# A decode step of attention and MLP on one core: the query weights loaded ahead of the MLP weights, and the queries made ahead of the MLP

## The chip, the cores and the metric

The kernel runs on one core of a Trainium2 chip. A core has five engines with their own instruction streams: TensorE (PE in the profile, its weight loads PEld), VectorE (DVE), ScalarE (ACT), GpSimd (POOL) and SyncE (SP), and 16 DMA engines that serve the queues of all of them. An engine takes its instructions in order; semaphores tie the engines together. The metric is the device time in microseconds.

## What is computed

One token x of 512 values is normalised, and two branches read the result xn. Branch A is attention over a cache: 32 heads of 128 values, each with its own keys and values, of which the last 4096 positions count. Branch B is a small MLP. The output is x plus the product of both.

```python
W = min(4096, max(256, Sk // 4))                 # 4096 of 32768 positions
q = (xn @ wq) per head                           # wq: 512 x 4096
p = softmax(q . k[:, Sk - W:, :] * 128 ** -0.5)
A = concat(p @ v[:, Sk - W:, :]) @ wo            # wo: 4096 x 512
h  = gelu(layernorm(xn) @ w1)
hs = concat(shifted quarters of h) @ w2          # one position only: every shift leaves zeros
x1 = xn + hs
B  = x1 + gelu(layernorm(x1) @ w3) @ w4          # w3: 512 x 1376, w4: 1376 x 512
out = x + A * silu(B)
```

With one position, the four shifts move h out of the sequence, so hs is a product of zeros with w2; the kernel carries it out with a zero vector. All tensors are bfloat16. Keys and values in the window are 32 MB each, wq and wo 4 MB each, the MLP weights 3.3 MB.

## The kernel before

**Loads.** All large loads are issued by SP through `load` (L77), which keeps them in program order. x comes twice through the ACT queue: `x_bf` (L81), spread over 128 partitions, and `x_row` (L84), four rows. SP issues w2, w3, w4 in three pieces, then wq (L85 to L94), each row of a partition contiguous: 4 KB for w2, 11 KB for w3, 32 KB for wq. Then follow, in a loop over pairs of heads s = 0 to 18, K of pair s (2 MB, a tile of 64 x 128 values in each partition) and V of pair s - 3. K has six buffers, V three. The V buffers lie where the weights were: the pool `wts` (w2, w3, w4, wq, and small tiles such as `sel`, `q_rows` and `hr`) is closed at s = 3 (L530), so the load of V0 waits until everything in `wts` has been read. As SP takes its instructions in order, K4 and all later loads stand behind V0.

**Ahead of the loop.** The statistics of x (`ln_stats`, L155: two products with a matrix of ones, short VectorE steps, a power on GpSimd) give `xn_f` and `xn_bf` (L179 to L185). The MLP follows: hs from w2 (L194), x1, the second statistics, `z3_bf` (L200), `a_ps` from w3 in 44 matmuls of one column (L212), Gelu on ScalarE, `hr_ps` in 15 matmuls of 512 columns with w2 and w4 (L220 and L223), a copy `hr`, the spreading over four rows `h2_ps` (L228 and L229), `bv`, and Silu into `g_row` (L233), which is used at the very end (L612). Then the queries: `qT_ps` in 128 matmuls of one column (L239), a transpose, `q_rows`, and `q_bc`, the queries of each pair spread over all partitions by four groups of four matmuls and four ScalarE copies (L248 to L253).

**In the loop.** Scores are made in two ways that share each K tile: of its 64 chunks of positions VectorE takes 32 or 40 in two halves (`k_vector`: the product with `q_bc`, L313, and a sum, L315), and TensorE the rest (`k_turn`: transposes, L328, which ScalarE copies, L329; `k_scores`, L334). The softmax works on two pairs at a time (`sm_*`), `v_pair` makes the weighted sums of the values (L431, L442), and the product with wo is gathered in `y_ps`. The loop is a region whose order on TensorE, VectorE and ScalarE is that of the program text. The instructions ahead of it are ordered by the scheduler, which may mix independent ones; the small masks and constants of L132 to L293 are put into gaps on VectorE in this way. All instructions ahead of the region come first on these three engines.

`ps_misc`, the PSUM pool of the MLP's and the queries' small results, has a single buffer, so each of them waits until the one before it has been read.

Of the kernel before, what the change touches and what calls it, by code (L numbers as in the profile page):

```python
# [8 lines left out]
P = 128  # L9
BF16 = mybir.dt.bfloat16  # L10
FP32 = mybir.dt.float32
# [18 lines left out]
def kernel(  # L30
# [14 lines left out]
    nc = tc.nc  # L45
# [3 lines left out]
    _, H, Sk, Dh = A_k_cache.shape  # L49
    HD = A_wq.shape[1]  # L50
# [5 lines left out]
    KC = D // P  # L56
# [9 lines left out]
    small = ctx.enter_context(tc.tile_pool(name="small", bufs=1))  # L66
    ps_misc = ctx.enter_context(tc.tile_pool(name="ps_misc", bufs=1, space=PSUM))
    ps_tr = ctx.enter_context(tc.tile_pool(name="ps_tr", bufs=3, space=PSUM))
# [6 lines left out]
    wts = wts_guard.__enter__()  # L75

    def load(dst, src):  # L77
        return tc.keep_in_program_order(nc.sync.dma_start(out=dst, in_=src))  # L78
# [3 lines left out]
    x_row = small.tile([P, P], BF16, name="x_row")  # L82
    nc.gpsimd.memset(x_row[:], 0.0)
    nc.scalar.dma_start(out=x_row[0:P:32, :], in_=A_x.rearrange("a b (j n) -> (a b j) n", j=KC))  # L84
    w2_sb = wts.tile([P, KC, D], BF16, name="w2_sb")  # L85
    load(w2_sb[:], B_w2.rearrange("(p c) n -> p c n", p=P))
    w3_sb = wts.tile([P, KC, F], BF16, name="w3_sb")
# [2 lines left out]
    load(w4_sb[:, 0:8, :], B_w4[0:8 * P, :].rearrange("(p c) n -> p c n", p=P))  # L90
    load(w4_sb[:, 8:10, :], B_w4[8 * P:10 * P, :].rearrange("(p c) n -> p c n", p=P))
    load(w4_sb[0:96, 10, :], B_w4[10 * P:F, :])
    wq_sb = wts.tile([P, KC, HD], BF16, name="wq_sb")
    load(wq_sb[:], A_wq.rearrange("(p c) n -> p c n", p=P))  # L94

    def load_kv(pool, cache, i, cuts=None):
        t = pool.tile([P, CP, Dh], BF16, tag="kv", name="kv")
# [9 lines left out]
    ident_bf = const.tile([P, P], BF16, name="ident_bf")  # L107
# [11 lines left out]
    sel = wts.tile([H, H // 2, P // 2, 2], BF16, name="sel")  # L119
# [9 lines left out]
    def make_masks(n):  # L129
        m = P // n  # L130
        blk = const.tile([P, m], BF16, name=f"blk{n}")
        nc.vector.tensor_reduce(out=blk[:], in_=ident_bf[:].rearrange("d (i t) -> d i t", t=n),  # L132
                                axis=AX.X, op=ALU.max)
        to = const.tile([P, n, m], BF16, name=f"to{n}")
        nc.vector.tensor_copy(out=to[:], in_=blk[:].unsqueeze(1).to_broadcast([P, n, m]))
        mt = const.tile([P, n], BF16, name=f"mt{n}")
        nc.vector.tensor_reduce(out=mt[:], in_=ident_bf[:].rearrange("d (i t) -> d t i", t=n),
                                axis=AX.X, op=ALU.max)
        mh = const.tile([P, n], FP32, name=f"mh{n}")
        nc.vector.tensor_reduce(out=mh[:], in_=ident_bf[:].rearrange("d (h i) -> d h i", h=n),  # L140
                                axis=AX.X, op=ALU.max)
        masks[n] = (to, mt, mh)
# [41 lines left out]
    xn_bf = small.tile([P, KC], BF16, name="xn_bf")  # L184
    nc.vector.tensor_copy(out=xn_bf[:], in_=xn_f[:])  # L185

    shifted_bf = small.tile([P, KC], BF16, name="shifted_bf")
    nc.vector.memset(shifted_bf[:], 0.0)  # L190
    hs_ps = ps_misc.tile([P, KC], FP32, tag="misc", name="hs_ps")
    for j in range(KC):
        for c in range(KC):
            nc.tensor.matmul(hs_ps[:, j:j + 1], lhsT=w2_sb[:, c, j::4],  # L194
                             rhs=shifted_bf[:, c:c + 1], start=(c == 0), stop=(c == KC - 1))
# [14 lines left out]
    for j, (m, cols) in enumerate(chunks):  # L210
        for c in range(KC):
            nc.tensor.matmul(a_ps[0:m, j:j + 1], lhsT=w3_sb[:, c, cols], rhs=z3_bf[:, c:c + 1],  # L212
                             start=(c == 0), stop=(c == KC - 1))
# [5 lines left out]
    for c in range(KC):  # L219
        nc.tensor.matmul(hr_ps[:], lhsT=shifted_bf[:, c:c + 1], rhs=w2_sb[:, c, :], start=(c == 0),  # L220
                         stop=False)
    for i, (m, _) in enumerate(chunks):
        nc.tensor.matmul(hr_ps[:], lhsT=a_bf[0:m, i:i + 1], rhs=w4_sb[0:m, i, :], start=False,  # L223
                         stop=(i == len(chunks) - 1))
# [7 lines left out]
    g_row = small.tile([P, P], FP32, name="g_row")  # L232
    nc.scalar.activation(out=g_row[:], in_=bv[:], func=ACT.Silu)  # L233


    qT_ps = ps_misc.tile([P, H], FP32, tag="misc", name="qT_ps")
    for h in range(H):
        for c in range(KC):
            nc.tensor.matmul(qT_ps[:, h:h + 1], lhsT=wq_sb[:, c, h * Dh:(h + 1) * Dh],  # L239
                             rhs=xn_bf[:, c:c + 1], start=(c == 0), stop=(c == KC - 1))  # L240
    qT_bf = small.tile([P, H], BF16, name="qT_bf")
    nc.vector.tensor_copy(out=qT_bf[:], in_=qT_ps[:])
    qr_ps = ps_misc.tile([H, Dh], BF16, tag="misc", name="qr_ps")
    nc.tensor.transpose(qr_ps[:], qT_bf[:], ident_bf[:])
    q_rows = wts.tile([H, Dh], BF16, name="q_rows")
    nc.vector.tensor_copy(out=q_rows[:], in_=qr_ps[:])
    q_bc = small.tile([P, H // 2, Dh], BF16, name="q_bc")
    for i in range(0, H // 2, 4):  # L248
        qb_ps = ps_tr.tile([P, 4, Dh], FP32, tag="pt", name="qb_ps")
        for k in range(4):  # L250
            nc.tensor.matmul(qb_ps[:, k, :], lhsT=sel[:, i + k, :, :].rearrange("k b a -> k (b a)"),
                             rhs=q_rows[:], start=True, stop=True)
        nc.scalar.copy(out=q_bc[:, i:i + 4, :], in_=qb_ps[:])  # L253
    make_masks(16)
    make_masks(8)

# [4 lines left out]
    for c in range(2):  # L261
        nc.vector.tensor_copy(
            out=few[:, c, 0:4 * NE].rearrange("p (a b) -> p a b", b=4),
            in_=ident_bf[:, 4 * NE * c:4 * NE * (c + 1)].rearrange("p (b a) -> p a b", b=4))
# [27 lines left out]
    for r in range(2):  # L292
        nc.vector.tensor_copy(out=pick_f[:, :, r, :],  # L293
                              in_=ident_bf[:, 32 * r:32 * r + 8].rearrange("p (i a) -> p i a", a=2))
# [230 lines left out]
    for s in range(NP + LAG):  # L525
        h = s - LAG
# [119 lines left out]
```

## Time and profile before

| | |
|---|---|
| median of 5 runs | 195.45 us (195.42 to 196.69) |
| profiled execution | 195.44 us, span of the core 193.6 us |
| busy share of the span: PE / DVE / ACT / POOL | 70% / 75% / 41% / 3% |
| DMA: bytes, queue of SP | 78.84 MB, 96.1% of 16 engines |
| chain that ended last | DMA 40%, DVE 37%, PE 11%, issue 3%, SP queue 3%, ACT 2% |

The span runs from the core's first instruction to its last; the rest of a run's time lies around it. In the profile's rows of slices each digit is the busy share of one fortieth of the span in tenths, and GB/s is what the DMA engines moved in it. A line of the timeline has start, duration, engine, line of the kernel, operation, output and inputs, and in brackets how long the engine stood idle before it and what ended that. A line of a DMA issue ends with the time from issue to landing. q1 is the queue of SP's loads, q10 that of ACT's.

### The profile page before, as it was taken

What the parts mean: (1) busy time and instruction counts of PE and PEld (TensorE: products, weight loads), DVE (VectorE), ACT (ScalarE), POOL (GpSimd) and SP (SyncE); (2) the same over time, 40 slices, a digit from 0 to 9 for tenths busy, and PEclk for the clock granted to TensorE, in tenths of its full rate; (3) what the DMA queues carried; (4) which work ended last, traced back from release to release, by engine and by line L of the source; (5) the groups of instructions that cost most, each with busy time, mean ns of one, the idle gap of its engine ahead of it and who ended that gap; (6) DMA issues with size and microseconds to landing.
All of it is one profiled execution on the core that took longest, in us unless ns stands there. A gap on an engine that the chain in (4) does not pass through costs nothing.

```text
span 193.6 us, 4727 instructions
## 1 busy us (share of the span) xinstructions
PE 136.4 (70%) x2108; PEld 105.4 (54%) x2108; DVE 145.3 (75%) x164; ACT 79.0 (41%) x173; POOL 6.2 (3%) x13
## 2 busy tenths in 40 slices
PE   0549779762687699497969944857757897958751
PEld 0444369652686663335959432247747546956640
DVE  1550108999999999999999999499999977792001
ACT  2003009882855460537359153161545028833000
POOL 2210006000000000000000000000000000000000
PEclk9999955975555556969555995795555579555555
DMA  6999899999999999999999999999999999999970
GB/s 211 407 507 433 372 427 433 430 422 427 433 427 427 427 418 430 427 433 433 427 430 423 430 430 430 430 433 423 427 433 427 433 428 432 416 437 416 411 309 3
DMA packets 7051, 79.13 MB, mean 409 GB/s; under 512 B 888, under 2 KB 1752, under 8 KB 2264
## 3 DMA queue, kind: packets, MB, share of 16 engines
q1 hardware_dynamic: 6880, 78.84, 96.1%
q8 instruction: 16, 0.26, 0.5%
q10 hardware_dynamic: 152, 0.00, 0.0%
q14 instruction: 3, 0.02, 0.0%
HBM read 78.84 MB, written 0.00 MB: 407 GB/s over the span
## 4 chain that ended last, share of the span: by engine, by line
DMA 40%; DVE 37%; PE 11%; issue 3%; SPq 3%; ACT 2%; POOL 1%; DVEq 0%; POOLq 0%
DMA kv<-in_A_k_cache_dram 31%; DVE S L315 22%; DVE prod L313 12%; DMA wo_rows<-in_A_wo_dram 7%; SPq L78 3%; PE hr_ps L223 2%; DMA x_bf<-in_A_x_dram 2%; ACT kt L329 2%; PE qT_ps L239 2%; PE oT L442 2%; PE a_ps L212 1%; PE oT L449 1%; PE hr_ps L220 1%; PE pt L328 1%; POOL ln_rstd_x L175 0%
## 5 line engine op out<-in xcount | busy, mean ns | idle before, releaser
L315 DVE TENSOR_REDUCE S<-prod 128x20 f32<-128x2560 bf16 (+1 forms) x32 | 83.8, 2620 | 1.1
L329 ACT COPY kt<-pt 128x1024 bf16<-128x1024 bf16 x54 | 51.0, 1021 | 22.8 <-PE pt L328 22.8
L313 DVE TENSOR_TENSOR prod<-kv,q_bc 128x2560 bf16<-128x2560 bf16 (+1 forms) x32 | 44.3, 1385 | 6.9 <-DMA kv<-in_A_k_cache_dram 4.6
L328 PE MATMUL pt<-ident_bf,kv 128*128 128x128 bf16 x432 | 40.2, 273 | 7.2 <-DMA kv<-in_A_k_cache_dram 5.3
L328 PEld LDWEIGHTS <-kv 128*128 128x128 bf16 x432 | 36.3, 127 | 10.7 <-DMA kv<-in_A_k_cache_dram 6.4
L442 PE MATMUL oT<-pT,kv 128*128 128x2 bf16 x768 | 22.5, 165 | 4.1 <-DMA kv<-in_A_v_cache_dram 4.1
L334 PE MATMUL sT<-qT_bf,kt 128*128 128x2 bf16 x432 | 17.5, 166 | 10.5 <-ACT kt L329 10.1
L442 PEld LDWEIGHTS <-kv 128*128 128x128 bf16 x768 | 21.6, 104 | 5.5 <-DMA kv<-in_A_v_cache_dram 5.4
L334 PEld LDWEIGHTS <-kt 128*128 128x128 bf16 x432 | 16.1, 104 | 13.1 <-ACT kt L329 12.3
L431 PE MATMUL ov<-kv,pT 128*8 128x512 bf16 x64 | 19.9, 481 | 0.0
L431 PEld LDWEIGHTS <-pT 128*8 128x8 bf16 x64 | 6.3, 103 | 12.3 <-issue 8.6
L371 PE MATMUL mb_ps<-md,par_t 4*128 4x4 f32 x16 | 4.3, 336 | 12.2 <-DVE md L363 12.2
L378 ACT ACTIVATE pT<-S,mb 128x64 bf16<-128x64 f32 x32 | 10.9, 357 | 0.2
L374 ACT COPY mb<-mb_ps 128x4 f32<-128x4 f32 x8 | 1.3, 162 | 23.2 <-PE mb_ps L371 23.2
L371 PEld LDWEIGHTS mb_ps<-md,par_t 4*128 4x128 f32 x16 | 3.8, 290 | 12.8 <-issue 12.2
L462 DVE TENSOR_TENSOR o<-oT,rden 128x2 bf16<-128x2 f32 x3 | 0.5, 160 | 10.7 <-PE oT L442 10.7
L466 ACT ACTIVATE o<-oT,rden 128x1 bf16<-128x1 f32 x26 | 4.7, 264 | 7.3 <-PE oT L449 5.3
L226 DVE COPY hr<-hr_ps 1x512 f32<-1x512 f32 x1 | 0.7, 679 | 8.8 <-PE hr_ps L223 8.8
L359 PE MATMUL mt_ps<-ident_f,m 128*2 128x128 f32 x8 | 2.8, 353 | 5.2 <-DVE m L353 5.2
L507 PE MATMUL yr_ps<-wo,ox 128*1 128x512 bf16 x16 | 6.1, 564 | 0.0
L378 ACT ACTIVATION_READ_ACCUMULATOR pT<-S,mb 128x1 f32 x32 | 6.0, 187 | 0.0
L157 PE MATMUL ln_ps<-x_f,ones_f 128*128 128x4 f32 x4 | 1.2, 365 | 5.9 <-DVE x_f L180 4.8
(116 smaller groups left out, 95.1 us busy)
## 6 DMA issues: line engine op xcount, KB each, us to landing
kv<-in_A_k_cache_dram SPq DMA_DIRECT2D x16, 2048.0 KB, 29.0
kv<-in_A_v_cache_dram SPq DMA_DIRECT2D x15, 2048.0 KB, 26.0
wq_sb<-in_A_wq_dram SPq DMA_DIRECT2D x1, 4096.0 KB, 17.7
wo<-in_A_wo_dram SPq DMA_DIRECT2D x1, 2048.0 KB, 27.1
w_sb<-in_B_w_dram SPq DMA_DIRECT2D x1, 1376.0 KB, 6.6
w_sb<-in_B_w_dram SPq DMA_DIRECT2D x1, 1024.0 KB
wo<-in_A_wo_dram SPq DMA_DIRECT2D x1, 1024.0 KB, 26.9
kv<-in_A_v_cache_dram SPq DMA_DIRECT2D x1, 1024.0 KB
```

Source lines behind the costliest of these rows:

```text
L78: return tc.keep_in_program_order(nc.sync.dma_start(out=dst, in_=src))
L313: nc.vector.tensor_tensor(out=prod[:, 0:m, :], in0=kn[:, rows, :], in1=q_bc[:, s:s + 1, :].to_broadcast([P, m, Dh]), op=ALU.mult)
L315: nc.vector.tensor_reduce(out=st[s // 2]["S"][:, s % 2, rows], in_=prod[:, 0:m, :], axis=AX.X, op=ALU.add)
L328: nc.tensor.transpose(pt[:, i, :], kn[:, n + b + i, :], ident_bf[:])
L329: nc.scalar.copy(out=kts[s][:, b:b + w, :], in_=pt[:, 0:w, :])
L334: nc.tensor.matmul(st[s // 2]["sT"][:, s % 2, c, :], lhsT=kt[:, c, :], rhs=qT_bf[:, 2 * s:2 * s + 2], start=True, stop=True)
L371: nc.tensor.matmul(mb_ps[:], lhsT=par_t[:].rearrange("k b a -> k (b a)"), rhs=md[:].rearrange("k r a -> k (r a)"), start=True, stop=True)
L378: nc.scalar.activation(out=s["pT"][:, i // 2, :, i % 2], in_=s["S"][:, i // 2, :], func=ACT.Exp, scale=scale, bias=mb[:, i:i + 1], accum_o ...
L431: nc.tensor.matmul(s["ov"][32 * r:32 * r + 8], lhsT=s["pT"][:, r, c:c + 4, :].rearrange("p i a -> p (i a)"), rhs=v[:, c:c + 4, :], start=F ...
L442: nc.tensor.matmul(s["oT"][:, 2 * r:2 * r + 2], lhsT=v[:, c, :], rhs=s["pT"][:, r, c, :], start=(c == 0), stop=(c == CP - 1))
L466: nc.scalar.mul(o_blk[b][:, c + k:c + k + 1], st[g]["oT"][:, hl + k:hl + k + 1], st[g]["rden"][:, hl + k:hl + k + 1])
L507: nc.tensor.matmul(yr_ps[:], lhsT=ox_blk[i][:, t:t + 1], rhs=wo_blk[i][:, t, :], start=(t == 0), stop=(t == n - 1))
```

## The change

Two blocks of the program text are moved; no operation is added or taken away. The load of wq goes ahead of those of w2, w3 and w4, and the queries ahead of the MLP.

```diff
     nc.scalar.dma_start(out=x_row[0:P:32, :], in_=A_x.rearrange("a b (j n) -> (a b j) n", j=KC))
+    wq_sb = wts.tile([P, KC, HD], BF16, name="wq_sb")
+    load(wq_sb[:], A_wq.rearrange("(p c) n -> p c n", p=P))
     w2_sb = wts.tile([P, KC, D], BF16, name="w2_sb")
     load(w2_sb[:], B_w2.rearrange("(p c) n -> p c n", p=P))
     w3_sb = wts.tile([P, KC, F], BF16, name="w3_sb")
...
     load(w4_sb[0:96, 10, :], B_w4[10 * P:F, :])
-    wq_sb = wts.tile([P, KC, HD], BF16, name="wq_sb")
-    load(wq_sb[:], A_wq.rearrange("(p c) n -> p c n", p=P))
...
     nc.vector.tensor_copy(out=xn_bf[:], in_=xn_f[:])
-    shifted_bf = small.tile([P, KC], BF16, name="shifted_bf")
...
-    g_row = small.tile([P, P], FP32, name="g_row")
-    nc.scalar.activation(out=g_row[:], in_=bv[:], func=ACT.Silu)
     qT_ps = ps_misc.tile([P, H], FP32, tag="misc", name="qT_ps")
...
         nc.scalar.copy(out=q_bc[:, i:i + 4, :], in_=qb_ps[:])
+    shifted_bf = small.tile([P, KC], BF16, name="shifted_bf")
...
+    g_row = small.tile([P, P], FP32, name="g_row")
+    nc.scalar.activation(out=g_row[:], in_=bv[:], func=ACT.Silu)
     make_masks(16)
     make_masks(8)
```

In the built program SP issues wq, w2, w3, the three pieces of w4, K0 to K3, and then as before. On TensorE the order is: statistics of x, qT, its transpose, twelve of the sixteen matmuls of `q_bc`, hs, the second statistics, the last four matmuls of `q_bc`, `a_ps`, `hr_ps`, `h2_ps`, and then the loop. On VectorE the copies of the queries come first, then the MLP's steps up to `bv`, then the first product of the loop. ScalarE makes the four copies into `q_bc`, then Gelu, then Silu, with the load of its function table ahead of each.

More of the change, by code (lines that the diff above doesn't have):

```diff
@@ L185 @@
     nc.vector.tensor_copy(out=xn_bf[:], in_=xn_f[:])
+    qT_ps = ps_misc.tile([P, H], FP32, tag="misc", name="qT_ps")
+    for h in range(H):
+        for c in range(KC):
+            nc.tensor.matmul(qT_ps[:, h:h + 1], lhsT=wq_sb[:, c, h * Dh:(h + 1) * Dh],
+                             rhs=xn_bf[:, c:c + 1], start=(c == 0), stop=(c == KC - 1))
+    qT_bf = small.tile([P, H], BF16, name="qT_bf")
+    nc.vector.tensor_copy(out=qT_bf[:], in_=qT_ps[:])
+    qr_ps = ps_misc.tile([H, Dh], BF16, tag="misc", name="qr_ps")
+    nc.tensor.transpose(qr_ps[:], qT_bf[:], ident_bf[:])
+    q_rows = wts.tile([H, Dh], BF16, name="q_rows")
+    nc.vector.tensor_copy(out=q_rows[:], in_=qr_ps[:])
+    q_bc = small.tile([P, H // 2, Dh], BF16, name="q_bc")
+    for i in range(0, H // 2, 4):
+        qb_ps = ps_tr.tile([P, 4, Dh], FP32, tag="pt", name="qb_ps")
+        for k in range(4):
+            nc.tensor.matmul(qb_ps[:, k, :], lhsT=sel[:, i + k, :, :].rearrange("k b a -> k (b a)"),
+                             rhs=q_rows[:], start=True, stop=True)
+        nc.scalar.copy(out=q_bc[:, i:i + 4, :], in_=qb_ps[:])
     shifted_bf = small.tile([P, KC], BF16, name="shifted_bf")
@@ L233 @@
     nc.scalar.activation(out=g_row[:], in_=bv[:], func=ACT.Silu)
[L236 to L253, printed above, removed]
     make_masks(16)
```

## The prediction
> **What bounds the kernel now.** I read the slices first, then the DMA totals, then the timeline of the first 31 us, then the waits late in the run.
>
> ```profile
> DVE  1550108999999999999999999499999977792001
> DMA  6999899999999999999999999999999999999970
> GB/s 211 407 507 433 372 427 433 430 422 427 433 427 427 427 418 430 427 433 433 427 430 423 430 430 430 430 433 423 427 433 427 433 428 432 416 437 416 411 309 3
> HBM read 78.84 MB, written 0.00 MB: 407 GB/s over the span
> ```
>
> (The DVE and DMA rows are 40 slices of 4.84 us.) The DMA row is full from the second slice to the last but two, at about 427 GB/s. 78.84 MB at 427 GB/s is 184.6 us; with the first data at 1.75 us and the last landing at about 189.2 us that fills the run. VectorE is full too, but only from 30 to 122 us; later it waits:
>
> ```profile
> 126.20 1.49 DVE L313 TENSOR_TENSOR prod<-kv,q_bc 128x2560 bf16<-128x2560 bf16 x1 [3.28 <-DMA kv<-in_A_k_cache_dram]
> ...
> 160.94 0.28 DVE L361 TENSOR_REDUCE mx<-mt_ps 2x2 f32<-2x128 f32 x1 [1.91 <-PE mt_ps L359]
> ...
> 165.47 1.23 DVE L313 TENSOR_TENSOR prod<-kv,q_bc 128x2048 bf16<-128x2048 bf16 x1 [0.61 <-DMA kv<-in_A_k_cache_dram]
> ...
> 182.48 1.87 PE L442 MATMUL oT<-pT,kv 128*128 128x2 bf16 x64 [1.04 <-DMA kv<-in_A_v_cache_dram]
> 185.51 1.01 PE L442 MATMUL oT<-pT,kv 128*128 128x2 bf16 x32 [1.16 <-DMA kv<-in_A_v_cache_dram]
> 189.32 0.38 PE L152 MATMUL y_ps<-wo_rows,o 128*1 128x128 bf16 x8 [0.30 <-DMA wo_rows<-in_A_wo_dram]
> ```
>
> The end hangs on the last bytes landing. The chain of waits gives VectorE 37% because it follows one released buffer backwards; the full DMA row says that the transfer so released then stood in a queue. So a change counts if it leaves the DMA engines without work, delays the consumers by more than these waits absorb, or changes the bytes. Bytes stay the same.
>
> **The change, part by part.** Now: MLP, then queries, then the first key product.
>
> ```profile
> 4.58 0.17 DVE L180 CAST x_f<-x_bf 128x4 f32<-128x4 bf16 x1 [3.32 <-DMA x_bf<-in_A_x_dram]
> 8.71 0.16 DVE L185 CAST xn_bf<-xn_f 128x4 bf16<-128x4 f32 x1
> 13.04 2.59 PE L212 MATMUL a_ps<-z_bf,w_sb 128*128 128x1 bf16 x44 [1.48 <-DVE z_bf L200]
> 23.19 0.29 DVE L231 TENSOR_TENSOR bv<-xn_row,h_ps 128x128 f32<-128x128 f32 x1 [0.66 <-PE h_ps L152]
> 23.54 3.50 PE L239 MATMUL qT_ps<-xn_bf,wq_sb 128*128 128x1 bf16 x128 [0.41 <-DVE bv L231]
> 27.64 0.21 DVE L246 COPY q_rows<-qr_ps 32x128 bf16<-32x128 bf16 x1 [0.38 <-PE qr_ps L244]
> 29.88 1.23 DVE L313 TENSOR_TENSOR prod<-kv,q_bc 128x2048 bf16<-128x2048 bf16 x1 [2.03 <-ACT q_bc L253]
> 30.54 0.54 SPq L78 DMA_DIRECT2D kv<-in_A_v_cache_dram  x1
> ```
>
> Here wq (4 MB) landed at 3.22 + 17.7 = 20.9 us, hidden behind the MLP. In the new order nothing useful hides it. PE and VectorE take their instructions in order, and in the built order q comes first, then the MLP (the fourth group of q_bc between the two statistics and a_ps), and the first key product stands behind bv. The early queries therefore can't start the attention early: it starts when the MLP is over.
>
> *When x arrives.* x_bf travels on the ACT queue beside the weights. All packets in a quarter of a microsecond from 3.25 us (number, MB, share of the engines):
>
> ```profile
> q1 hardware_dynamic: 24, 0.10, 97.2%
> q10 hardware_dynamic: 25, 0.00, 5.5%
> ```
>
> q10 carries x, q1 the SP loads: they alternate one for one. w2's packets are 4 KB, x_bf has 8 rows and a completion on each of 16 engines, and it lands at about 4.56 us. Their place is taken by wq's rows of 4 x 4096 bf16 values, 32 KB: at 27 GB/s (427/16) 1.2 us each, and the eight on an engine are the whole of wq. So x_bf should land about with wq. The Trainium skill ("DMA: Bandwidth & Descriptors", "Queues, rings and completion order") says that an engine drains a packet of some 9 to 17 descriptors from one queue before it switches. By that rule x_bf's eight rows go in one turn, at about 4.5 us if its turn comes first and after wq if not. I take the trace's one-for-one. 4.19 MB are through at 11.7 us by the running sum of the trace's GB/s; the lag of the slowest engine and the completion make it 12.5 us. If the rule's early turn is right, x costs nothing and the chain below is 4.3 us shorter.
>
> *The chain to the end of the MLP*, from x landing: statistics to xn_bf 4.3 (4.56 to 8.87); qT to q_rows 4.35 (23.5 to 27.85); twelve of the sixteen broadcast matmuls 2.2 (2.66 for all, less 4 x 0.117); hs 0.7; x1 0.2; the second statistics 3.8 (as the first); z_bf to h2 10.15 (12.98 to 23.13). Sum 25.7, so h2 ends at 38.2 us, and the first key product starts at 38.6 instead of 29.9: **8.7 us late**. The fourth q_bc group hides in the 1.4 us PE gap ahead of a_ps; the Gelu and Silu table loads (1.28 us each) stay hidden behind the second statistics and hr. One part is open: hr's 15 matmuls took 0.43 us each although the profile's clock says 1.0. "TensorE: Matmul & The Clock Gate" (section "What you observe") has the rate double after some 4 us of sustained matmuls; at half of 0.43 hr would take 3.2 instead of the 5.9 us measured, and the chain would be 2.7 shorter. In the trace PE worked from 13.0 us and the spacing still was 0.43 us at 20.6, so I keep the slow rate.
>
> *The queue past which the load is moved.* The five MLP loads move behind wq; the four key loads wait for semaphores that x_bf, the first weight load, x_row and the next load release, so they are issued at some 12.5 us and after, while 3.3 MB (7.8 us) are queued: no hole. V0 needs the weights' room, so it waits for the last reader. That was the last q_bc matmul (issue at 30.54), and is now h2 (38.2). All other loads stand behind V0 on SP. From first issue (0.72) to first data (1.75) is 1.03 us, so V0 moves from 39.2 us. What must cover that is K3, the last of the queued loads:
>
> ```profile
> kv<-in_A_k_cache_dram SPq DMA_DIRECT2D x1, 2048.0 KB, 34.1
> ```
>
> Issued at 7.8 us (the fourth of the key loads from 4.58 on), landed at 41.9. Less 0.4 for its completion and 0.4 for the earlier start below, the slowest engine runs dry at 41.1: V0 comes 1.9 us in time. The next tight ones are V3 to V6, which wait for attention, so for the 8.7 us. V6 goes at 88.0 now, while K9 ahead of it lands at 77.7 + 22.7 = 100.4; at 96.7 + 1.0 it is 2.7 us in time. V3 to V5 have 4 us or more.
>
> *Where the 8.7 us go.* VectorE's waits of 3.28, 0.44, 0.25, 1.91 and 0.61 us after 122 us take 6.5 of them. The rest, 2.2, meets PE's waits for values in the tail (0.62, 1.04, 1.16, 0.82: 3.6 us). Nothing reaches the end, with 1.4 us to spare.
>
> *What can be gained.* From 1.75 to 3.00 us the engines had 0.68 of their share and 164 GB/s, with small packets. A large first load may fill this: 0.32 x 1.25 = 0.4 us by share, (1 - 164/430) x 1.25 = 0.8 by bytes, or nothing if it is start-up latency. I take 0.3, near the share, with the loss through alternation taken off.
>
> **Sum.** The profiled run took 195.44 us (span 193.6, 1.84 outside), the median is 195.45, so no correction. 195.44 - 0.3 = **195.1 us**.
>
> **Rivals.**
> 1. *x_bf isn't held back* (the page's early turn), or hr runs warm: the attention starts some 4 to 6 us late instead of 8.7. Against the first speaks the one-for-one row. The time is the same, 195.1: it is hidden anyway.
> 2. *The new wait reaches the end* (slower). The MLP is longer than 25.7 by more than the cover: beyond 1.4 us VectorE's lateness passes PE's tail, beyond 1.9 the DMA engines stand idle ahead of V0, and from there each us costs one. A chain of 29 us gives 197. For it: several steps are put together from places where they had other neighbours, and PE had unexplained gaps (0.59 us at 28.17). Against it: hr may be faster.
> 3. *The start gains more* (faster): 0.8 us from the bytes, and a tail without lag; 194.3. Little speaks for it, since only 1.25 us is open.
> 4. *The queries free the attention early*: K0 lands at 25.8, 4 us ahead of its first use now. Excluded by the order on VectorE, and worth nothing while the DMA row is full.
>
> **How the numbers follow.** A measurement of this kernel tells about 0.5% (1 us) from no change. My forecast 0.60, rival 1 0.12 (both same), rival 2 0.20, rival 3 0.08. The range goes from the gain by bytes (194.6) to a chain that is some 3 us too long (197.0). Faster 0.08, same 0.72, slower 0.20.
>
> **What would show it.** x_f starts at 12 to 13 us instead of 4.58; qT at about 17; first key product near 38.6; V0 issued near 38.2 with the DMA row unbroken about 40 us; the waits after 122 us shorter; the last values still landing near 189. I am wrong if a slice of the DMA row falls below 9 between 35 and 100 us, or if PE no longer waits for values at the end.

## The result

The changed kernel takes 196.76 us (median of 28 runs, 195.52 to 198.05), the kernel before 195.46 us (49 runs, 195.32 to 196.88): ratio 1.0058, 95% interval 1.0044 to 1.0073. Ratios are of the means and leave out slow runs, more than 1.5% above the fastest of the same kernel; of all runs told here these are two of 201.5 us, of the kernel with only the load moved. It is slower by 1.1 us by the means and 1.3 by the medians, and its runs scatter over 2.5 us, where 41 of the 49 of the kernel before keep within 0.3 and eight lie near 196.6. The forecast was 195.1 us, "same"; the time fell into the range, on the slower side.

The timeline of the changed kernel's first 40 us, with the lines that answer to those shown of the kernel before (start, duration, engine, line, operation, what it waited for):

```profile
13.23 0.17 DVE L180 CAST x_f<-x_bf 128x4 f32<-128x4 bf16 x1 [11.97 <-DMA x_bf<-in_A_x_dram]
17.36 0.16 DVE L185 CAST xn_bf<-xn_f 128x4 bf16<-128x4 f32 x1
17.57 3.55 PE L191 MATMUL qT_ps<-xn_bf,wq_sb 128*128 128x1 bf16 x128 [1.91 <-DVE xn_bf L185]
21.73 0.21 DVE L198 COPY q_rows<-qr_ps 32x128 bf16<-32x128 bf16 x1 [0.38 <-PE qr_ps L196]
27.73 2.58 PE L232 MATMUL a_ps<-z_bf,w_sb 128*128 128x1 bf16 x44 [0.81 <-DVE z_bf L220]
37.51 0.53 SPq L78 DMA_DIRECT2D kv<-in_A_v_cache_dram  x1
37.52 0.29 DVE L251 TENSOR_TENSOR bv<-xn_row,h_ps 128x128 f32<-128x128 f32 x1 [0.66 <-PE h_ps L152]
37.73 1.22 DVE L314 TENSOR_TENSOR prod<-kv,q_bc 128x2048 bf16<-128x2048 bf16 x1
```

x lands 8.7 us later than before, the queries are begun only then although the kernel is meant to make them early, and the first key product starts at 37.7 us instead of 29.9. So far this is the chain of the prediction. The rows of slices on the page of the changed kernel (here a slice is 4.87 us), and how its page divides the chain of work that ended last:

```profile
DVE  0017120499999999999999999999999999992001
DMA  6999999999999999999999999999999999999970
GB/s 242 404 404 423 444 427 430 424 424 429 424 430 430 424 427 425 430 424 430 434 370 424 430 427 427 430 430 430 427 430 427 430 430 430 412 442 420 407 282 4
DVE 61%; DMA 13%; PE 11%; issue 6%; ACT 4%; SPq 1%; POOL 1%; POOLq 0%
```

VectorE now has no pause until its work is done: the waits that the kernel before had after 122 us are used up, as forecast. One of them is left in the timeline, and TensorE still waits for values at the end:

```profile
166.78 1.23 DVE L314 TENSOR_TENSOR prod<-kv,q_bc 128x2048 bf16<-128x2048 bf16 x1 [0.17 <-DMA kv<-in_A_k_cache_dram]
...
183.72 1.87 PE L443 MATMUL oT<-pT,kv 128*128 128x2 bf16 x64 [0.99 <-DMA kv<-in_A_v_cache_dram]
186.86 1.01 PE L443 MATMUL oT<-pT,kv 128*128 128x2 bf16 x32 [1.27 <-DMA kv<-in_A_v_cache_dram]
190.68 0.38 PE L152 MATMUL y_ps<-wo_rows,o 128*1 128x128 bf16 x8 [0.30 <-DMA wo_rows<-in_A_wo_dram]
```

So TensorE still waits for the last bytes, only 1.36 us later (190.68 against 189.32). The new thing is one slice of the GB/s row, the 21st, with 370 among neighbours of 424 to 434: from 97.4 to 102.3 us the DMA engines had too little to do. (427 - 370) / 427 x 4.87 = 0.65 us of transfer are missing there. The DMA row reads 9 in that slice too: the sign that the prediction named, a slice of it below 9, is too coarse for such a gap.

### The profile page after: what moved, and what is told of

It reads as the page before. It is cut to its first block, busy times and chain, and to the rows that moved or that the text cites. A ratio compares the mean times of both kernels' runs of the same rounds, so it can differ in the third digit from the quotient of the medians.

```text
span 194.9 us, 4728 instructions
## 1 busy us (share of the span) xinstructions
PE 132.6 (68%) x2108; PEld 102.7 (53%) x2108; DVE 145.5 (75%) x164; ACT 80.2 (41%) x174; POOL 6.3 (3%) x13
## 4 chain that ended last, share of the span: by engine, by line
DVE 61%; DMA 13%; PE 11%; issue 6%; ACT 4%; SPq 1%; POOL 1%; POOLq 0%
DVE S L316 37%; DVE prod L314 19%; DMA wo_rows<-in_A_wo_dram 7%; DMA x_bf<-in_A_x_dram 6%; ACT kt L330 4%; PE yr_ps L508 3%; PE hr_ps L243 2%; PE oT L443 2%; SPq L78 1%; PE a_ps L232 1%; PE hr_ps L240 1%; DVE m L354 1%; DVE mx L362 1%; DVE S L350 1%; PE pt L329 1%
## 5 line engine op out<-in xcount | busy, mean ns | idle before, releaser
L329 PE MATMUL pt<-ident_bf,kv 128*128 128x128 bf16 x432 | 39.5, 270 | 1.9 <-ACT kt L330 1.9
L329 PEld LDWEIGHTS <-kv 128*128 128x128 bf16 x432 | 35.9, 126 | 5.0 <-issue 4.8
L335 PE MATMUL sT<-qT_bf,kt 128*128 128x2 bf16 x432 | 17.3, 166 | 10.7 <-ACT kt L330 10.3
L443 PEld LDWEIGHTS <-kv 128*128 128x128 bf16 x768 | 21.4, 103 | 5.5 <-DMA kv<-in_A_v_cache_dram 5.4
L335 PEld LDWEIGHTS <-kt 128*128 128x128 bf16 x432 | 15.9, 103 | 13.4 <-ACT kt L330 12.6
L432 PE MATMUL ov<-kv,pT 128*8 128x512 bf16 x64 | 20.7, 494 | 0.0
L205 ACT CAST q_bc<-qb_ps 128x512 bf16<-128x512 f32 x4 | 2.1, 592 | 21.8 <-PE qb_ps L203 21.8
L372 PEld LDWEIGHTS mb_ps<-md,par_t 4*128 4x128 f32 x16 | 3.4, 265 | 14.0 <-issue 13.2
L463 DVE TENSOR_TENSOR o<-oT,rden 128x2 bf16<-128x2 f32 x3 | 0.5, 159 | 10.7 <-PE oT L443 10.7
L157 PEld LDWEIGHTS ln_ps<-x_f,ones_f 128*128 128x128 f32 x4 | 1.0, 310 | 13.8 <-DVE x_f L180 13.5
```

The source lines that it names most:

```text
L329: nc.tensor.transpose(pt[:, i, :], kn[:, n + b + i, :], ident_bf[:])
L335: nc.tensor.matmul(st[s // 2]["sT"][:, s % 2, c, :], lhsT=kt[:, c, :], rhs=qT_bf[:, 2 * s:2 * s + 2], start=True, stop=True)
L372: nc.tensor.matmul(mb_ps[:], lhsT=par_t[:].rearrange("k b a -> k (b a)"), rhs=md[:].rearrange("k r a -> k (r a)"), start=True, stop=True)
L432: nc.tensor.matmul(s["ov"][32 * r:32 * r + 8], lhsT=s["pT"][:, r, c:c + 4, :].rearrange("p i a -> p (i a)"), rhs=v[:, c:c + 4, :], start=F ...
L443: nc.tensor.matmul(s["oT"][:, 2 * r:2 * r + 2], lhsT=v[:, c, :], rhs=s["pT"][:, r, c, :], start=(c == 0), stop=(c == CP - 1))
```

## The experiments

Two theories were put against each other. **G, the gap:** x is late because its packets alternate with wq's long rows, everything behind it is late, and in the end a V load (V6 is that of pair 6) is issued so late that the DMA engines run short. **L, the load order:** the large load in front serves the DMA engines worse in itself.

### wq in shorter rows, and w2 ahead of wq

Four loads of 8 KB rows in place of one of 32 KB rows; nothing else differs from the changed kernel.

```diff
-    load(wq_sb[:], A_wq.rearrange("(p c) n -> p c n", p=P))
+    for c in range(KC):
+        load(wq_sb[:, c, :], A_wq.rearrange("(p c) n -> p c n", p=P)[:, c, :])
```

> The changed kernel, with the load of wq cut into four loads of 1 MB whose rows are 8 KB instead of 32 KB; nothing else. Theory G (late V load): x is late because its packets alternate with wq's long rows, everything behind it is late, and in the end V6 is issued so late (97.2 us) that the DMA engines run short at 98 to 100 us. Then here x_f starts at 5 to 6 us, qT is bound by wq's landing at about 13, the first key product comes at about 33.5 us (37.7 in the changed kernel, 29.9 before), V6 goes at about 93, the GB/s row has no slice under 410 between 40 and 160 us, and the time is 195.3 to 195.8 us. Theory L (load order): the large load in front serves the DMA engines worse, whatever the rest does: 196.5 us or more.

195.46 us, ratio 0.9991 (0.9980 to 1.0002), 22 runs between 195.24 and 195.60: the loss is gone. The first key product starts at 33.2 us, V6 is issued at 92.58. G holds, L in this form falls.

In a second kernel wq stays one load, but w2 goes ahead of it.

```diff
+    w2_sb = wts.tile([P, KC, D], BF16, name="w2_sb")
+    load(w2_sb[:], B_w2.rearrange("(p c) n -> p c n", p=P))
     wq_sb = wts.tile([P, KC, HD], BF16, name="wq_sb")
     load(wq_sb[:], A_wq.rearrange("(p c) n -> p c n", p=P))
```

> The changed kernel with w2 loaded ahead of wq; wq stays one load of 32 KB rows. x's packets alternate with w2's 4 KB rows as in the kernel before. Theory G: x_f at about 4.6 us, wq lands at about 13.5, first key product at about 33.7, V6 at about 93, no gap, 195.3 to 195.8 us. Theory L: 196.5 us, since wq's long rows still stand ahead of most of the weights.

195.41 us, ratio 0.9992 (0.9980 to 1.0005). x_f starts at 4.61 us, the first key product at 35.1 (1.4 later than expected, qT ran from 14.24), V6 at 93.22. The order "queries ahead of the MLP" costs nothing as long as x is in time.

The third tests the alternation by itself: wq in two loads of 16 KB rows.

```diff
-    for c in range(KC):
-        load(wq_sb[:, c, :], A_wq.rearrange("(p c) n -> p c n", p=P)[:, c, :])
+    for c in range(0, KC, 2):
+        load(wq_sb[:, c:c + 2, :], A_wq.rearrange("(p c) n -> p c n", p=P)[:, c:c + 2, :])
```

> The changed kernel with wq in two pieces whose rows are 16 KB. x_f started at 4.58 us beside 4 KB rows, 6.19 beside 8 KB rows and 13.2 beside 32 KB rows. If x's packets alternate one for one with the rows, x_f starts at 8 to 9 us here (eight rows of 0.6 us). If x is served in one turn, at 4.6 to 6.2 or not before the first piece has landed whatever the row size. The time is no test here: qT is bound by the landing of wq at about 13 us, so about 195.5 us.

The conversions of x in the timelines of the kernels with 8 KB and with 16 KB rows:

```profile
6.19 0.17 DVE L181 CAST x_f<-x_bf 128x4 f32<-128x4 bf16 x1 [4.92 <-DMA x_bf<-in_A_x_dram]
```
```profile
8.48 0.17 DVE L181 CAST x_f<-x_bf 128x4 f32<-128x4 bf16 x1 [7.22 <-DMA x_bf<-in_A_x_dram]
```

With rows of 4, 8, 16 and 32 KB, x_f starts at 4.6, 6.2, 8.5 and 13.2 us: some 0.3 us for each KB, which is eight rows of 1 KB at 27 GB/s. This alone does not show the alternation: each of the four first loads has eight rows on an engine, so x served in one turn behind the whole first load would give the same slope. The packets of the changed kernel from 7 to 8 us decide it:

```profile
q1 hardware_dynamic: 16, 0.52, 126.7%
q10 hardware_dynamic: 16, 0.00, 0.8%
```

From 3.5 to 12 us 112 packets went on each of the two queues. x, 1 KB in all, is served one packet for one row. (The time of this kernel's single run, 195.93 us, says little.)

### The buffer that V6 waits for

V6 stands on SP until `v_pair` has read V3's buffer. In the groups named in MOVED this step is 16 matmuls of 512 columns, in the others 64 narrow ones.

```diff
-MOVED = (1, 3)
+MOVED = (3,)
```

> The changed kernel with MOVED = (3,): the second group of heads makes its weighted sums by 64 narrow matmuls (1.9 us a pair) instead of 16 wide ones (5 to 6.3 us), so the buffer that V6 waits for is free some 4.5 us sooner; x and the MLP are as late as in the changed kernel. Theory G: V6 goes at about 93, the gap at 98 to 100 us is gone, 195.3 to 195.8 us and the runs lie close together. Theory L, or a lateness that reaches the end in another place: 196.5 us or more.

195.88 us, ratio 1.0028 (1.0011 to 1.0046). x_f and the first key product are as late as in the changed kernel (13.33 and 37.38), V6 goes at 92.42, and the row of slices has no gap. Half of the loss is gone, not all: most runs lie between 195.5 and 196.2, some at 197.

The control, the same edit on the kernel before:

> The kernel before with MOVED = (3,): the control of the same edit on the changed kernel. V6 has cover to spare here (issue 88.0, engines short from about 98). Theory G: no effect, 195.3 to 195.6 us; what the edit gives the changed kernel is then the gap at V6. Theory L or a plain gain from the narrow matmuls: the same gain as on the changed kernel, about 0.6 us, so 194.9 us or less.

195.46 us, ratio 1.0009 (0.9990 to 1.0027): no effect, where V6 has time to spare. Its profile is of a run of 196.65 us, one of six that lie between 196.6 and 197.1. It has no gap later, but 7.08 MB moved by 20 us where the profile before has 7.54, a delay of 1.1 us, and wq lands 19.0 us after its issue instead of 17.7. Its cause is open; it may be that of the longer runs of the kernel before too, and it is another scatter than that of the changed kernel, whose four profiles all have 11.70 to 11.73 MB at 30 us, near the 11.75 of the kernel before.

Another way to the same end: four V buffers and five K buffers, in the same room.

```diff
-K_BUFS = 6
+K_BUFS = 5
-V_BUFS = 3
+V_BUFS = 4
```

> The changed kernel with four V buffers and five K buffers (the same room). V6 takes the buffer of V2 instead of V3 and so doesn't wait for the second wide v_pair: V6 at about 90 us unless a K load ahead of it on the queue waits longer. x and the first key product as late as in the changed kernel. Theory G: no gap at 98 to 102 us, 195.4 to 195.9 us. Theory L: 196.5 us or more.

195.29 us, ratio 0.9997 (0.9980 to 1.0014), with x_f at 13.29 and the first key product at 37.93, as late as ever. V6 goes at 84.7, and the row of slices has no gap. So the loss of the changed kernel is gone although the lateness is still there. Whether lateness costs nothing at all is not shown by this: the kernel before with the same buffers takes 195.00 us (below), 0.3 us less by the medians, with intervals that overlap.

To look for the other half, V0 was relieved as well: MOVED = (3,) and the row hr out of the weights' pool.

```diff
-    hr = wts.tile([1, D], FP32, name="hr")
+    hr = small.tile([1, D], FP32, name="hr")
```

> The changed kernel with MOVED = (3,) and, in addition, the row hr in another pool than the weights, so that V0 waits for the last matmul of hr (about 36.1) and not for h2 (37.5). With MOVED = (3,) alone 195.88 us were left. If the rest is V0's small cover: 195.4 to 195.6 us. If it is another thing (the start of the loads, lateness at V3 to V5 or at the end): 195.9 us as before.

195.75 us, ratio 1.0016 (0.9994 to 1.0038), V0 at 35.3. One of 13 runs lies above 196.2, where seven of 22 did with MOVED = (3,) alone; but the median is between the two expectations and the intervals overlap, so this doesn't decide.

### The same kernel three times more

> The changed kernel again, one profile. Theory G: the later V6 is issued (before 96 us no loss, at 97.2 some 0.6 us of data missing by 104 us), the longer the run; 195.5 us with V6 early, 197 to 198 with V6 at 98 or later. Theory L: the time doesn't go with V6; the data is missing elsewhere.

> As the repeat ahead of it: with V6 at 96 or earlier 195.5 us, at 97 to 98 us 196.5 to 197.5 and GB/s below 400 about 98 to 101 us.

> As the repeats ahead of it: with V6 at 96 or earlier 195.5 us, at 97 to 98 us 196.5 to 197.5 and GB/s below 400 about 98 to 101 us.

The times were 196.76, 195.52 and 195.60 us, with V6 at 96.73, 96.37 and 96.13. In the second and third the stretch about 100 us has no gap. The windows of two us of the first profile of the changed kernel (196.71 us), then of the second repeat; the last column is GB/s, the one ahead of it the DMA engines' share:

```profile
96.00:98.00 2.00, 2.00 (x21) 1.14 (x20) 1.97 (x2) 0.77 (x2) 0.00 (x0) 0.90 0.97 418
98.00:100.00 2.00, 1.40 (x30) 1.23 (x27) 2.00 (x3) 2.00 (x3) 0.00 (x0) 1.00 0.94 320
100.00:102.00 2.00, 1.44 (x57) 1.35 (x55) 1.97 (x2) 0.93 (x2) 0.00 (x0) 1.00 1.00 401
```
```profile
96.00:98.00 2.00, 1.96 (x29) 1.61 (x27) 2.00 (x1) 1.62 (x3) 0.00 (x0) 1.00 1.01 434
98.00:100.00 2.00, 0.87 (x23) 0.70 (x24) 1.97 (x4) 1.77 (x2) 0.00 (x0) 1.00 1.02 426
100.00:102.00 2.00, 2.00 (x76) 2.00 (x72) 2.00 (x1) 0.30 (x1) 0.00 (x0) 1.00 0.98 418
```

V6's issue in the two:

```profile
97.22 0.54 SPq L78 DMA_DIRECT2D kv<-in_A_v_cache_dram  x1
```
```profile
96.37 0.54 SPq L78 DMA_DIRECT2D kv<-in_A_v_cache_dram  x1
```

0.85 us decide between a gap and none. The first repeat was long although V6 was not the latest. Its row of slices, and its windows about 40 us, show the gap in another place:

```profile
GB/s 229 417 409 420 439 427 430 427 360 429 427 430 430 430 397 430 425 427 434 430 413 427 430 427 427 430 434 430 434 424 427 434 427 430 413 444 424 399 311 4
...
38.00:40.00 2.00, 1.82 (x33) 1.48 (x33) 1.52 (x3) 1.24 (x3) 1.53 (x1) 1.00 0.98 410
40.00:42.00 2.00, 1.27 (x29) 1.10 (x29) 2.00 (x1) 2.00 (x3) 1.97 (x1) 1.00 0.92 311
42.00:44.00 2.00, 1.44 (x28) 1.35 (x26) 1.93 (x3) 0.88 (x2) 0.00 (x0) 0.81 1.02 434
```

Here it was V0, issued at 38.44 us; in the other three it went at 36.8 to 37.5. What differs ahead of it is x (13.60 against 13.23 to 13.33) and hr. The eleven matmuls of hr with w4 in the first repeat and in the third:

```profile
32.67 4.40 PE L243 MATMUL hr_ps<-w_sb,a_bf 128*1 128x512 bf16 x11
```
```profile
32.34 3.10 PE L243 MATMUL hr_ps<-w_sb,a_bf 128*1 128x512 bf16 x11
```

The spacing of these matmuls halves, from 0.43 to 0.22 us, somewhere in hr, in each run at another one; the two wide `v_pair` steps ahead of V6 likewise took 5.5 and 6.3 us in the first profile, 5.6 and 4.9 in the first repeat, and 5.0 and 6.0 in the second and third. So one kernel has two places where about a us decides. This fits the scatter, though only four of its runs have a trace; theory G holds with V0 beside V6.

A rival is that VectorE, which no longer pauses and has 61% of the last chain, has become the bound. The last product of the loop in the first profile and in the third repeat:

```profile
170.90 1.22 DVE L314 TENSOR_TENSOR prod<-kv,q_bc 128x2048 bf16<-128x2048 bf16 x1
```
```profile
170.79 1.22 DVE L314 TENSOR_TENSOR prod<-kv,q_bc 128x2048 bf16<-128x2048 bf16 x1
```

VectorE is equally late in both, and has 61% of the chain in both, yet the third repeat took 195.60 us and the first profile 196.71. What differs is V6's issue and the gap, and a rest that stays open (below).

### Lateness without x or long rows

The four-piece kernel, with matmuls with the zero vector put ahead of hr. They add to the MLP's time and nothing to its sum.

```diff
-    for c in range(KC):
-        nc.tensor.matmul(hr_ps[:], lhsT=shifted_bf[:, c:c + 1], rhs=w2_sb[:, c, :], start=(c == 0),
-                         stop=False)
+    for c in range(KC + 10):                     # then KC + 21, KC + 40
+        nc.tensor.matmul(hr_ps[:], lhsT=shifted_bf[:, c % KC:c % KC + 1], rhs=w2_sb[:, c % KC, :],
+                         start=(c == 0), stop=False)
```

> The kernel with wq in four pieces (195.46 us, first key product at 33.3, V6 at 92.6), and ten more matmuls with the zero vector at the head of hr, which add 10 x 0.43 = 4.3 us to the MLP's chain and nothing to its sum. x and the loads stay as in the four-piece kernel. Theory G (lateness alone makes the loss, by way of V6): first key product at about 37.6, V6 at about 97, GB/s falls near 98 to 100 us, 196 to 197.5 us and scattered. Theory L (wq's long rows or x's place make the loss): 195.5 us, close together.

195.49 us, ratio 0.9987 (0.9970 to 1.0004). The dose was too small: the ten matmuls cost 2.1 us, not 4.3, because the faster spacing came within them and the eleven of hr with w4 then took 2.54 us instead of 3.57; V6 went at 93.58, in time.

> The four-piece kernel with 21 more matmuls with the zero vector instead of ten; the earlier ten cost only 2.1 us[...], so eleven more should add 11 x 0.216 = 2.4 us. First key product at 37.7, as late as in the changed kernel, with x at 6.2 us and no row over 8 KB ahead of it. Theory G (lateness alone): V6 at 96 to 97.2, GB/s below 400 in a stretch of 98 to 100 us, runs scattered over 1 us or more, 195.8 to 197 us. Theory L (the long rows, or x beside them): 195.5 us with little scatter, as with ten.

First key product at 37.92, V6 at 96.73. 195.60 us, ratio 1.0015 (0.9990 to 1.0041), runs from 195.28 to 197.86: half of them at 195.5, the others scattered upward over 2 us. The scatter is G's, the median is between the theories: V6 sits on the edge here, V0 too (37.71).

> The same with 40 more matmuls: another 19 x 0.216 = 4.1 us, first key product at 41.8, V0 issued at 41.6. The engines ran short at 39.5 us and were back at full rate some 2.3 us after the issue when V0 went at 41.94. Theory G: a gap of some 4 us ahead of V0 and about 199 us, whatever the loads are like. Theory L: 195.5 us.

200.31 us, ratio 1.0252 (1.0220 to 1.0284), V0 at 42.38; the slice there moved 96 GB/s. x was at 6.2 us, and the first key product did not start at 41.8 as expected but at 27.6: in this build it stands ahead of hr's copy. So neither x nor the start of attention is late here, the second key product (40.7) and V0 are, and the gap stands ahead of V0.

### One half of the change each

The load order alone (wq ahead of w2, MLP ahead of the queries), and the order of the computation alone (the loads as before).

> The kernel before with only the load of wq moved to the front; the MLP is still made ahead of the queries. Both theories: x_f at 13.2 us, first key product at about 38.5 (8.6 late), V0 at 39. Theory G: V6 at about 97, a gap as in the changed kernel, 196.3 to 197.5 us, scattered over 1 us or more. Theory L: 196.7 us with even loss and no gap at V6.

Median 199.42 us of six runs; the four that the ratio counts took 198.19 to 199.62, ratio 1.0159 (1.0118 to 1.0199), longer than expected. The profile is of a run of 201.54 us, so it is not taken for the others: in it x_f started at 13.54, the first key product 3 us later than expected (the second statistics ended 10.1 us after x instead of 8.4, behind mask instructions on VectorE, and a pause of 1.36 us, without a cause in the trace, stood ahead of q_bc), V0 went at 42.40, and the slice there moved 66 GB/s.

> The kernel before with only the queries moved ahead of the MLP; the loads as before. x_f at 4.6 us, qT starts when wq has landed at 20.9, and 21.4 us of chain behind it end the MLP at about 42.3; the first key product is 12 us late, V0 goes at 42, after K3 has landed. Theory G: a gap at 41 to 44 us and another near V6 (100 us), 198 to 201 us. Theory L: the load order is the old one, 195.5 us.

199.36 us, ratio 1.0179 (1.0148 to 1.0211). V0 at 41.94. The expected lateness of the first key product did not come: in this build VectorE had two key products ahead of hr's copy (at 31.0 us), and V6 went at 94.35 with no gap. The whole loss is the gap ahead of V0: the slice from 39.5 to 44.5 us moved 80 GB/s instead of 427, which is 4.0 us of transfer, and the median is 3.9 us longer. Windows of one us:

```profile
38.00:39.00 1.00, 1.00 (x6) 0.40 (x5) 0.00 (x0) 0.00 (x0) 0.00 (x0) 1.00 0.99 426
39.00:40.00 1.00, 1.00 (x12) 0.56 (x11) 0.39 (x1) 0.11 (x1) 0.00 (x0) 1.00 0.66 279
40.00:41.00 1.00, 0.79 (x15) 0.67 (x13) 1.00 (x2) 1.00 (x2) 0.00 (x0) 1.00 0.15 66
...
43.00:44.00 1.00, 0.44 (x16) 0.35 (x13) 0.96 (x2) 0.98 (x2) 1.00 (x1) 1.00 0.67 131
44.00:45.00 1.00, 1.00 (x23) 1.00 (x20) 1.00 (x1) 0.99 (x2) 1.00 (x1) 1.00 1.08 393
```

The engines run short within the 40th us, and are back at their rate some 2.1 to 2.5 us after the issue at 41.94. By these ends V0 would have to be issued by about 37.3 us for an unbroken stream. The missing bytes give a later time: 41.94 less 4.0 is 37.9 us, and the first repeat, with a slice of 360 GB/s at V0's issue of 38.44, gives 37.7 in the same way.

### Is there a faster version?

The kernel before and the four-piece kernel, each with four V and five K buffers.

> The kernel before with four V and five K buffers. If the buffers only took away V6's wait, which the kernel before has cover for: 195.4 us. If they help at the end, where the last V loads wait for a buffer: 195.0 us, as the fast half of the changed kernel's runs with them.

> The four-piece kernel (x in time, queries first) with four V and five K buffers. No gap at V0 (issue at about 33) and none at V6: 195.4 us if the buffers only took away a wait, 195.0 us if they help at the end; the runs close together in both cases.

195.00 us, ratio 0.9978 (0.9955 to 1.0001), and 195.49 us, ratio 0.9997 (0.9988 to 1.0007). The first has ten of 14 runs at 194.9 to 195.1, below the fastest run of the kernel before beside it (195.34), but its interval touches 1, and the second shows no gain from the same edit. No version is clearly faster. One thing differs, though nothing here was built to test it: of the 63 runs of kernels with wq's load and the queries ahead, x in time and no gap (four pieces, w2 first, four pieces with ten more matmuls, four pieces with four V buffers; not counting the single run with 16 KB rows) none lies above 195.73 us, while eight of the 49 runs of the kernel before lie near 196.6.

## Why the prediction was wrong

**x.** Forecast at 12.5 us, measured 13.2, and the alternation is shown by the four row sizes and the packet counts. Of the two readings, the Trainium skill's turn of 9 to 17 descriptors ("DMA: Bandwidth & Descriptors", "Queues, rings and completion order") and the trace's one for one, the trace was right.

**The chain.** Forecast 25.7 us from x to h2; it took 24.3 (13.2 to 37.5). hr took 5.5 us in the first profile and 4.8 to 6.1 in the repeats, against 5.9 taken. The prediction's reading that all 15 matmuls took 0.43 us each was wrong: fifteen of these make 6.4 us, and in the trace before the spacing halves at about 21.0 us, just behind the place that was read. The doubling of the rate that the Trainium skill puts after some 4 us of sustained matmuls ("TensorE: Matmul & The Clock Gate", "What you observe") came within hr in all four profiles, some 3 to 5 us after its start (an estimate from the lengths of hr and the two spacings). First key product 37.7 against 38.6, V0 37.5 against 38.2.

**Where the lateness goes.** Forecast: VectorE's waits and TensorE's waits for values take it all. They did: one wait of 0.17 us in place of the 6.5, and TensorE still waits at the end. The second and third repeat (195.52 and 195.60 us) and the kernel with more V buffers are as late, and lose little or nothing.

**The step that failed** is the cover of the moved queue: "the slowest engine runs dry at 41.1: V0 comes 1.9 us in time", and with the same reckoning V6 "2.7 us in time". Two terms of it were mis-sized.
1. *When the engines run dry.* It was taken from the landing of the last queued load, K3 at 41.9 us in a run where V0 was already queued behind it. In the run where nothing followed, the data stopped at 39.5 to 40. Summing the bytes (15.9 MB ahead of V0) in the trace before gives 39.7 us, a number that was at hand.
2. *How soon a load brings data.* The 1.03 us from the first issue to the first packet were taken; to full rate it is more than 2 us after an empty queue, and counted by the missing bytes it is worth a standstill of some 1.8 us (41.94 + 1.8 - 39.7 = 4.0).

Together the cover was 2 to 3 us too large: the prediction's sum lets V0 go until 40.1 us (41.1 less 1.0), the runs until 37.3 to 37.9. The profiles with V0 at 37.5 and 37.7 show no gap yet, the one at 38.44 does. The same reckoning holds for V6, an estimate: 41.1 MB stand ahead of it, through at 98.3 us in the trace before, so it has to go by 96.0 to 96.5; 96.1, 96.4 and 96.7 show no gap, 97.2 does. The forecast issues, 38.2 and 96.7, lay past or on these edges, and not 2 us inside. V6's own issue was also 0.5 us later than forecast, since the two wide `v_pair` steps took 11.8 us together where they took 10.7 before.

**The gain at the start** of 0.3 us is not there. The window from 1.75 to 3.00 us is full now (419 GB/s where it was 164), but by 30 us the changed kernel had moved 11.70 MB and the kernel before 11.75 (sums of GB/s in windows of one us); that the start was only waiting for its first data remains likely, and was not tried.

**The rivals.** Rival 2 had the mechanism, the price of one us per us and the right place for V0; V6, the other place, stands in the prediction among those that are in time. That the lateness passes TensorE's tail, the other half of rival 2, did not happen. Rival 1 was the case of the four-piece kernel, at its forecast cost of nothing. Rival 3 fell.

**What stays open.** In the first profile the stretches from 96 to 104 and from 104 to 120 us are slower than those of the second repeat by 27 and 9 GB/s (395 against 422, 424 against 433), together 0.36 MB or 0.85 us of the 1.19 us between the two; the second stretch has no wait that I could name, and its 0.14 MB is less than one row of 16 KB on each engine (0.26 MB), which the edges of a window alone can move. The rest I did not find. How the loss divides between V0 and V6 over all runs isn't settled either: relieving V6 brought the ratio from 1.0058 to 1.0028 in one way and to 0.9997 in the other, where the buffers also help the kernel before.

## What to carry to other kernels

- Where the DMA queue is the bound, reckon the cover of a delayed load from the bytes queued ahead of it, not from the landing of the last one, and take off the time to full rate (here over 2 us), not to the first packet. A forecast of "1.9 us in time" over a chain of 25 us is no cover.
- A tiny load beside a large one on another queue was served row by row with it here: give it a neighbour with short rows (here w2's 4 KB), and look at what the first load's row length is.
- Lateness of the consumers cost little or nothing by itself here, up to 8 us; look for the one load that waits on it at the head of an in-order queue.

## What was not expected of the hardware

- The landing of 1 KB in 128 rows of 8 bytes was delayed in proportion to the row length of the other queue's load: 4.6, 6.2, 8.5 and 13.2 us for 4, 8, 16 and 32 KB.
- The spacing of matmuls of 512 columns changed from 0.43 to 0.22 us in the middle of hr, at another one in each run, while the profile's clock row showed full speed from the start: ten added ones cost 2.1 us, and the eleven of hr with w4 took between 3.1 and 4.4 us in four runs of one kernel.
